# Decode attention on one core: one spread product for a pair of heads, four heads turned at once, and three of eight value parts weighted and folded ahead of the keys' last sum

## The chip, the cores and the metric

The kernel runs on one core of a Trainium2 chip. Its time is the device time of one execution in microseconds (us); the kernel before takes 2681.38 us in the median of three runs (2681.13 to 2682.27). The core has TensorE (PE in the profile, its weight loads PEld), VectorE (DVE), ScalarE (ACT), GpSimd (POOL) and SyncE (SP), which here only issues transfers; 16 DMA engines carry these. SBUF is the large memory on the core, in 128 partitions; TensorE writes its products to banks of PSUM, a second memory.

## The reference, cut to what matters

```python
def _A_ref(x, k_cache, v_cache, wq, wo):        # B=2, Sq=1, D=576, H=32, Sk=8192, Dh=128
    q = (x @ wq).reshape(B, Sq, H, Dh).transpose(0, 2, 1, 3)
    scores = jnp.einsum("bhqd,bhkd->bhqk", q, k_cache) * (Dh ** -0.5)
    p = _softmax(scores, axis=-1)
    o = jnp.einsum("bhqk,bhkd->bhqd", p, v_cache)
    return o.transpose(0, 2, 1, 3).reshape(B, Sq, H * Dh) @ wo

x = x + _A_ref(_layernorm(x), A_k_cache, A_v_cache, A_wq, A_wo)
x = x + _B_ref(_layernorm(x), B_w_gate, B_w_up, B_w_down)      # gated MLP, 4608 wide
x = x + _A_ref(_layernorm(x), A_k_cache, A_v_cache, A_wq, A_wo)
x = x + _B_ref(_layernorm(x), B_w_gate, B_w_up, B_w_down)
```

All is float32. Each of the two attention layers reads the whole key and value caches, 268 MB each, once; with the weights 1152 MB come from HBM in a run.

## The kernel before

**Items and parts.** The work of a layer is a list ITEMS of 30 pairs (two neighbouring heads h, h+1 of one batch entry b) and four single heads at the end. For a pair, the 128 partitions hold 64 stretches of each head, 128 keys to a partition. Keys and values of a pair are 8 parts of 16 rows (a row: 128 numbers of one key in each partition). The first layer takes the items in order, the second in reverse (`seq`), so that the two batch entries of a pair of heads follow each other and some data at the turn is kept.

**Where things lie.** `space` is one SBUF tile of 200 KB a partition, shared out by the class Arena while the program is written: in the long loops there are three places of 8 parts. A list of transfers (`plan_first`, `plan_second`, `plan_mlp`) is fixed in order: keys of item n+1, values of item n, keys of n+2, and so on. `done(key)` gives a part back, and `pump()` issues the next transfers on SP's queue as far as their places are free; on the chip each waits there, in order, for the last reader of its place. A transfer of keys thus waits for the values of an earlier item, and one of values for the keys of the item before.

**One item.** `query(n)` spreads the item's q over the partitions: one TensorE product for each head of the pair, from 4 rows of `qsb` with a column of `pick`, into a PSUM bank (`qb`). `multiply(n, k, m)` takes m parts from part k: VectorE multiplies keys by q (L743, one operand in SBUF, one in the bank), GpSimd adds the upper half of each row's 128 products to the lower (L772). `add_up` sums the 64 left (VectorE, L775) into the scores and gives the keys' parts back. `units(n)` makes three steps of a pair: parts 0 to 2, 3 to 5, 6 and 7 (48, 48 and 32 rows). The last sum of item p, with the search for its maximum (`peak`, L799, a turn on TensorE, L801), stands at the head of the next item's turn in the loop over `seq`. Then `highest` (L807, L809) and `softmax` (ScalarE, L832) write the weights into `prz`, SBUF, one copy for all pairs. `total` and `inverse` make 1 / sum.

**Values.** `values(i)` multiplies four rows of values at a time by their weights on TensorE (L913) into an accumulator in PSUM. For most pairs (`folds(n)`: n from 3 to 26 in the first layer, from 2 to 26 in the second) the last FOLD = 2 of the 8 parts go another way, two items later (item f in the loop): `weigh(f)` adds the two halves of the weights in `prz` into `share` in PSUM (L875, both operands in SBUF), multiplies the parts by them in place (VectorE, L880, one operand in SBUF and one in PSUM) and adds row upon row on GpSimd until four are left (L883). `folded(f)` brings these into the accumulator with one call of a product (L891, two instructions), gives the parts back and with them the place of the values.

**Closing a pair of heads.** After both batch entries (item a in the loop), `gather` takes the diagonal of the accumulator (L927, L928) into the tile `wide`, `context` turns it with four products (L936, two instructions each) into `po`, and `divide` writes the four quotients into `oT`, mostly on ScalarE (L955).

**The order** is written out by hand in the loop over `seq` and is that of every engine's instructions. For a pair it was: last sum and peak of p; weigh(f); first multiply; query of the next item; highest and softmax of p; second multiply; total and inverse; folded(f); gather and context of a; values of p; first sum; third multiply; second sum; divide of a.

**q itself** is made by `q_products` in 9 steps: the 2048 columns of a half row of `wq` go to four strips of 32 partitions, 512 columns each, strip c holding heads 4c to 4c+3 of the 16. A row of a strip is a batch entry and a half of the heads. `spread()` fills `wide` with the pattern that `norm` needs; `home` is an SBUF tile that holds kept rows at the turn of the layers.

Of the kernel before, what the change touches and what calls it, by code (L numbers as in the profile page):

```python
# [15 lines left out]
P = 128  # L16
B = 2
H = 32
SK = 8192
DH = 128  # L20
# [5 lines left out]
HALF = P // 2  # L26

GH = 4
WIDE = (GH, 4 * GH)
NU = 9  # L30
EQ = 512
HG = DF // 16
PAD = 6
# [12 lines left out]
SPLIT = (18, 18, 12, 16)  # L46
FOLD = 2

# [77 lines left out]
def decode_layers(ctx, tc, x_in, kc, vc, wq, wo, wg, wu, wd, out):  # L126
    nc = tc.nc
# [288 lines left out]
    def plan_mlp(layer):  # L416
# [24 lines left out]
    make_identity(nc, ident)  # L441
    sizes = [1, 1, 4, 4, 4, 4, 2, 24, 4]
    few = consts.tile([P, sum(sizes)], F32, name="few")
    unit, mhalf, pick, diag, of, sums, side, owner, strip = [
        few[:, sum(sizes[:k]):sum(sizes[:k + 1])] for k in range(len(sizes))
# [161 lines left out]
    def attention(layer):  # L607
# [4 lines left out]
        def q_products(w, at, to, start, stop):  # L612

            for c in range(4):
                nc.tensor.matmul(
                    acc[32 * c:32 * c + 2 * B, to, :], xt[:, PAD + at:PAD + at + 2 * B], w[:, c, :],
                    start=start, stop=stop,
                )

        def half_products(h):  # L620

            for k in range(4):
                key = ("wq", 1, h, k)
                q_products(
                    ready.pop(key).rearrange("p (c w) -> p c w", w=EQ), 64 * k + 8 + 4 * h, h,
                    k == 0, h == 0 and k == 3,
                )
                done(key)
                if k > 0 if h else k < 3:
                    idle_products(2, 1 - h)  # L630

        if layer == 0:
            for us in GU[0]:
                w = ready.pop(("wq", 0, us[0])).rearrange("p (u c w) -> p u c w", c=4, w=EQ)
                for u in us:
                    q_products(w[:, u - us[0]], 32 * u, 0, u == 0, u == NU - 1)
                done(("wq", 0, us[0]))
        else:
            half_products(1)
            key = ("wq", 1, NU - 1)  # L640
            q_products(ready.pop(key).rearrange("p (c w) -> p c w", w=EQ), 32 * (NU - 1), 1, False, True)
            done(key)
# [5 lines left out]
        seq = list(range(N))[::1 - 2 * layer]  # L648

        def query(n):  # L650

            it = ITEMS[n]
            qps.append(qps.pop(0))
            qb[n] = qps[0]
            for i in range(it.heads):
                h, to = it.h + i, slice(i * HALF, i * HALF + P // it.heads)
                c, r = (h // 4) % 4, h // 16 * B + it.b
                nc.tensor.matmul(  # L658
                    qb[n][to, :], pick[32 * c:32 * c + 4, r:r + 1].to_broadcast([4, P // it.heads]),
                    qsb[32 * c:32 * c + 4, (h % 4) * DH:(h % 4 + 1) * DH], start=True, stop=True,  # L660
                )

# [4 lines left out]
        def at_once(n, k):  # L667

            return layer == 1 and n == seq[0] and k in (0, ITEMS[n].parts - 1)
# [229 lines left out]
        def values(i, lo=0, hi=8):  # L899
# [20 lines left out]
            if left and 4 * hi >= gs and not less:  # L920
                ready.pop(key)

        def gather(n):

            t = osb[n] = wide
            q = accumulator(n).rearrange("p (r d) -> p r d", r=4)
            nc.vector.tensor_tensor(out=q, in0=q, in1=diag.unsqueeze(2).to_broadcast([P, 4, DH]), op=ALU.mult)  # L927
            nc.vector.tensor_reduce(out=t, in_=q.rearrange("p r d -> p d r"), axis=AX.X, op=ALU.add)  # L928

        def context(n):  # L930

            lo = 32 * (ITEMS[n].h % GH)
            t = osb.pop(n)
            for i in range(GH):
                c = 2 * ITEMS[n].heads
                nc.tensor.matmul(po[lo:lo + 32, i, :c], t[:, i::GH], of[:, :c], start=True, stop=True)  # L936

        def divide(n, by_scalar=False):
            it = ITEMS[n]
            lo = 32 * (it.h % GH)  # L940
            if it.heads == 1:
# [6 lines left out]
                )  # L948
                return
            for b, i in ((b, i) for b in range(B) for i in range(2)):  # L950
                to = oT[lo + 32 * i:lo + 32 * i + 32, it.h // GH, :, :, b]
                o = po[lo:lo + 32, :, 2 * b + i:2 * b + i + 1].to_broadcast([32, GH, 2])
# [43 lines left out]
        for i, n in enumerate(seq):  # L996
# [254 lines left out]
```

## Time and profile before

| | before |
|---|---|
| time, median of three runs | 2681.38 us (2681.13 to 2682.27) |
| the profiled execution, span | 2681.6 us, 15416 instructions |
| busy: DVE, POOL, PE, ACT | 1992.5, 1560.5, 885.1, 165.7 us |
| read from HBM | 1152.39 MB, 430 GB/s over the span |
| share of the DMA queue of SP on the 16 engines | 99.7% |
| first attention layer, its long loop | about 45 to 1140 us |
| MLP and the turn to the second layer | about 1285 to 1400 us |
| second attention layer, its long loop | about 1465 to 2541 us |

How to read it. The page gives the busy time of each engine, the span in 40 slices, the DMA queues, the chain of work that ended last and the costliest groups of instructions. A group's line has the kernel's line, the engine, the operation, the tiles written <- read, the shapes and the count; then busy us and the mean ns of one; then the idle time just before them and what ended it. A row of the timeline has its start and its length in us, and in square brackets how long the engine had stood idle and what released it. "DMA share" in a table by windows is the busy share of the 16 DMA engines. The rows for SPq are the requests for transfers at the moment when they leave SP's queue.

### The profile page before, as it was taken

Reading aid. Unit: us, or ns where it says so; the run is one execution under the profiler, and the core shown is the slowest. Engines: PE = TensorE matmul, PEld = TensorE weight load, DVE = VectorE, ACT = ScalarE, POOL = GpSimd, SP = SyncE. Lnnn points to the kernel's source line nnn. Section 1 sums busy time; section 2 is a strip of 40 time slices with the busy share of each in tenths; the row PEclk is TensorE's granted clock in tenths of the full one; section 3 lists DMA queues with packets and bytes.
Section 4 is the critical chain, followed back from the end, with each engine's and each line's share of the span. In section 5 each row is a group of like instructions: output and inputs, shape, how many; then the busy total and the mean of one; then the engine's idle time right before and its main releaser. Section 6 shows DMA issues by size and latency. Waiting matters only on the chain.

```text
span 2681.6 us, 15416 instructions
## 1 busy us (share of the span) xinstructions
PE 885.1 (33%) x6198; PEld 270.4 (10%) x6198; DVE 1992.5 (74%) x907; ACT 165.7 (6%) x792; POOL 1560.5 (58%) x412
## 2 busy tenths in 40 slices
PE   1323332232223232334663323233223323332346
PEld 0000000000000000011221000000000000000022
DVE  4878888888788888867038778878888888888740
ACT  0000000000000000001026000000000000000000
POOL 2546676667666766744028457666766676676620
PEclk8556655665566566566986665566566556655678
DMA  9999999999999999999999999999999999999998
GB/s 422 436 437 427 434 434 431 436 430 435 432 431 433 431 437 433 429 430 427 417 417 426 434 432 432 435 435 430 431 435 433 432 432 435 434 428 434 433 428 378
DMA packets 29344, 1153.41 MB, mean 430 GB/s; under 512 B 3384, under 2 KB 3416, under 8 KB 4184
## 3 DMA queue, kind: packets, MB, share of 16 engines
q1 hardware_dynamic: 29088, 1152.40, 99.7%
q8 instruction: 49, 0.80, 0.1%
q14 instruction: 23, 0.19, 0.0%
q10 hardware_dynamic: 184, 0.02, 0.0%
HBM read 1152.39 MB, written 0.01 MB: 430 GB/s over the span
## 4 chain that ended last, share of the span: by engine, by line
DMA 67%; DVE 20%; PE 8%; POOL 2%; ACT 2%; issue 1%; SPq 0%; POOLq 0%; ACTq 0%; DVEq 0%
DMA space<-in_A_k_cache_dram 60%; DVE space L743 17%; PE acc L891 3%; DMA space<-in_B_w_down_dram 3%; DMA space<-in_B_w_gate_dram 2%; POOL space L772 2%; DVE scores L775 2%; PE bank L658 1%; DMA space<-in_B_w_up_dram 1%; PE bank L809 1%; ACT prz L832 1%; DMA space<-in_A_v_cache_dram 1%; PE bank L845 1%; PE acc L913 0%; PE bank L1210 0%
## 5 line engine op out<-in xcount | busy, mean ns | idle before, releaser
L772 POOL TENSOR_TENSOR space<-space 128x3072 f32<-128x3072 f32 (+4 forms) x221 | 1128.2, 5105 | 461.3 <-DVE space L743 330.9
L743 DVE TENSOR_TENSOR space<-space,bank 128x6144 f32<-128x6144 f32 (+4 forms) x223 | 1111.9, 4987 | 346.1 <-DMA space<-in_A_k_cache_dram 274.6
L775 DVE TENSOR_REDUCE scores<-space 128x48 f32<-128x3072 f32 (+4 forms) x223 | 568.7, 2550 | 93.1 <-POOL space L772 92.9
L913 PE MATMUL acc<-space,prz 128*16 128x512 f32 (+1 forms) x3312 | 513.7, 785 | 353.9 <-DMA space<-in_A_v_cache_dram 342.3
L883 POOL TENSOR_TENSOR space<-space 128x2048 f32<-128x2048 f32 x147 | 398.0, 2708 | 392.6 <-DVE space L880 377.0
L658 PE MATMUL bank<-qsb,few 4*64 4x128 f32 (+1 forms) x256 | 45.5, 433 | 895.0 <-DVE space L743 887.4
L880 DVE TENSOR_TENSOR space<-space,bank 128x4096 f32<-128x4096 f32 x49 | 216.6, 4420 | 1.7
L913 PEld LDWEIGHTS acc<-space,prz 128*16 128x16 f32 (+1 forms) x3312 | 108.7, 117 | 740.3 <-issue 454.0
L824 ACT ACTIVATE nbs<-bank 128x2 f32<-128x2 f32 (+1 forms) x68 | 11.6, 171 | 2012.5 <-PE bank L809 1975.4
L658 PEld LDWEIGHTS bank<-qsb,few 4*64 4x64 f32 (+1 forms) x256 | 20.2, 199 | 914.6 <-DVE space L743 897.9
L580 POOL TENSOR_TENSOR rstd<-ve,few 128x1 f32<-128x1 f32 x4 | 2.2, 551 | 168.3 <-DVE ve L578 168.3
L891 PE MATMUL acc<-space,few 128*16 128x512 f32 x98 | 92.6, 1048 | 0.7 <-POOL space L883 0.7
L801 PE MATMUL bank<-ident,m 128*1 128x128 f32 x68 | 21.1, 310 | 196.5 <-DVE m L799 196.2
L936 PE MATMUL bank<-few,wide 128*32 128x4 f32 (+1 forms) x272 | 20.9, 200 | 170.5 <-DVE wide L928 170.5
L1162 DVE STREAM_TRANSPOSE gu<-acc 128x288 f32<-128x288 f32 x4 | 1.9, 483 | 93.0 <-ACT acc L1160 93.0
L832 ACT ACTIVATE prz<-scores,nbs 64x128 f32<-64x128 f32 (+1 forms) x128 | 50.7, 396 | 11.7 <-POOL prz L822 8.9
L765 ACT ACTIVATE space<-space 128x128 f32<-128x128 f32 x164 | 48.4, 296 | 19.4 <-DVE space L743 16.4
L809 PE MATMUL bank<-m,few 1*128 1x2 f32 (+1 forms) x136 | 38.8, 352 | 26.9 <-DVE m L807 26.9
L584 DVE TENSOR_TENSOR x<-bank,x 128x144 f32<-128x144 f32 x4 | 1.2, 308 | 60.5 <-PE bank L1210 41.5
L927 DVE TENSOR_TENSOR acc<-acc,few 128x512 f32<-128x512 f32 x34 | 23.5, 691 | 26.7 <-PE acc L913 26.7
L936 PEld LDWEIGHTS bank<-few,wide 128*32 128x32 f32 x272 | 19.0, 154 | 216.6 <-issue 211.6
L759 POOL TENSOR_TENSOR space<-space,qs 128x512 f32<-128x512 f32 x23 | 29.2, 1271 | 18.5 <-ACT qs L740 18.5
(106 smaller groups left out, 498.2 us busy)
## 6 DMA issues: line engine op xcount, KB each, us to landing
space<-in_A_v_cache_dram SPq DMA_DIRECT2D x7, 4096.0 KB
space<-in_A_k_cache_dram SPq DMA_DIRECT2D x6, 4096.0 KB
space<-in_B_w_gate_dram SPq DMA_DIRECT2D x9, 1152.0 KB
space<-in_B_w_up_dram SPq DMA_DIRECT2D x9, 1152.0 KB
space<-in_B_w_down_dram SPq DMA_DIRECT2D x8, 1152.0 KB
space<-in_A_wq_dram SPq DMA_DIRECT2D x9, 1024.0 KB
space<-in_A_wo_dram SPq DMA_DIRECT2D x2, 4608.0 KB
space<-in_A_k_cache_dram SPq DMA_DIRECT2D x4, 2048.0 KB
```

Source lines behind the costliest of these rows:

```text
L658: nc.tensor.matmul(qb[n][to, :], pick[32 * c:32 * c + 4, r:r + 1].to_broadcast([4, P // it.heads]), qsb[32 * c:32 * c + 4, (h % 4) * DH:(h ...
L743: nc.vector.tensor_tensor(out=u[:, :r, :], in0=t[:, :r, :], in1=qb[n].unsqueeze(1).to_broadcast([P, r, DH]), op=ALU.mult)
L765: nc.scalar.activation(u[:, j, :], u[:, j, :], AF.Copy, accum_out=S[n][:, base(n, k) + j:base(n, k) + j + 1])
L772: nc.gpsimd.tensor_tensor(out=half, in0=half, in1=u[:, :r, DH // 2:], op=ALU.add)
L775: nc.vector.tensor_reduce(out=S[n][:, base(n, k):base(n, k) + own_rows(n, k, m)], in_=prod.pop((n, k)), axis=AX.X, op=ALU.add)
L809: nc.tensor.matmul(mT[n][:, :heads], ones[0:1, :], m1[:, :heads], start=True, stop=True)
L832: nc.scalar.activation(pr[at, lo:].rearrange("p (g e) -> p g e", e=4)[:, 0:it.rows // 2 * it.heads:2 * it.heads, :], s[at, :it.rows].rearr ...
L880: nc.vector.tensor_tensor(out=t, in0=t, in1=share.unsqueeze(2).to_broadcast([P, rows, DH]), op=ALU.mult)
L883: nc.gpsimd.tensor_tensor(out=t[:, :rows - less], in0=t[:, :rows - less], in1=t[:, less:rows], op=ALU.add)
L891: nc.tensor.matmul(accumulator(n)[0:16, :], owner[:, 8 * ITEMS[n].b:8 * ITEMS[n].b + 16], part_at(arena.live[key, lo][0], 4 * DH), start=F ...
L913: nc.tensor.matmul(accumulator(n)[32 * c:32 * c + m, :], pr[:, at:at + m], t[g // 4][:, g % 4 * 4:g % 4 * 4 + 4, :].rearrange("p j d -> p ...
L936: nc.tensor.matmul(po[lo:lo + 32, i, :c], t[:, i::GH], of[:, :c], start=True, stop=True)
```

## The change

It has four pieces.

1. **q by one product.** The strips of `wq` are read in another order (`by_strips`), so that the two heads of a pair stand in neighbouring strips, in the same columns. The two products of `query` become one over 36 rows (4 of each strip and the 28 between). Its stationary side, which sends the first head to partitions 0 to 63 and the second to 64 to 127, is made by `pairs_of` with two VectorE copies whenever the half of the heads changes (twice in a layer), from the new constant `both`, into `wide` and a third of `home`.
2. **Four heads turned at once.** For heads below 28, `gather` of two neighbouring pairs goes side by side into `home`; `context` runs only at the second of them, with 64 columns where it had 32, and `divide` writes the quotients of both.
3. **Three parts folded.** FOLD is 3: the weighting takes 48 rows where it took 32, GpSimd folds 48 to 24, 12, 8 and 4 rows, and TensorE multiplies five parts instead of six.
4. **The order.** `weigh(f)` stands ahead of the last sum and the peak of p, and `folded(f)` right behind the first multiply and the query.

```diff
-FOLD = 2
+FOLD = 3
...
+    both = both.rearrange("p (r i) -> p r i", i=2)
+    low_rows, high_rows = [
+        ident[:, HALF * q:HALF * (q + 1)].rearrange("p (i z) -> p z i", i=2)[:, :4, :] for q in range(2)
+    ]
+    nc.vector.tensor_add(both, low_rows, high_rows)
...
-                    acc[32 * c:32 * c + 2 * B, to, :], xt[:, PAD + at:PAD + at + 2 * B], w[:, c, :],
+                    acc[32 * c:32 * c + 2 * B, to, :], xt[:, PAD + at:PAD + at + 2 * B], w[:, c // 2, c % 2],
...
+        def by_strips(w):
+
+            return w.rearrange("p (a q m e d) -> p q e a m d", a=2, q=2, m=2, e=2)
...
+        of_batch = [wide, home[:, 2 * P:3 * P]]
+        spread_for = []
+
+        def pairs_of(s):
+
+            if spread_for[-1:] == [s]:
+                return
+            spread_for.append(s)
+            for b, to in enumerate(of_batch):
+                nc.vector.tensor_copy(
+                    to.rearrange("p (i q) -> p i q", i=2), both[:, s * B + b, :].unsqueeze(2).to_broadcast([P, 2, HALF])
+                )
...
-            for i in range(it.heads):
-                h, to = it.h + i, slice(i * HALF, i * HALF + P // it.heads)
-                c, r = (h // 4) % 4, h // 16 * B + it.b
-                nc.tensor.matmul(
-                    qb[n][to, :], pick[32 * c:32 * c + 4, r:r + 1].to_broadcast([4, P // it.heads]),
-                    qsb[32 * c:32 * c + 4, (h % 4) * DH:(h % 4 + 1) * DH], start=True, stop=True,
-                )
+            h, r = it.h, it.h // 16 * B + it.b
+            lo = HALF * (h // 4 % 2) + 32 * (h % 2)
+            m = h // 8 % 2 * 2 + h % 4 // 2
+            if it.heads == 2:
+                rows = slice(lo, lo + 36)
+                pairs_of(it.h // 16)
+                of_row = of_batch[it.b][rows, :]
+            else:
+                rows = slice(lo, lo + 4)
+                of_row = pick[rows, r:r + 1].to_broadcast([4, P])
+            nc.tensor.matmul(qb[n], of_row, qsb[rows, m * DH:(m + 1) * DH], start=True, stop=True)
...
+        def joined(n):
+
+            return ITEMS[n].h < H - GH
+
+        def closes(n):
+
+            return ITEMS[n].h % GH == 2 - 2 * layer
+
         def gather(n):
 
-            t = osb[n] = wide
+            at = ITEMS[n].h % GH * HALF
+            t = osb[n] = home[:, at:at + P] if joined(n) else home[:, :P] if layer else wide
...
+            if joined(n):
+                if not closes(n):
+                    return
+                t = home[:, :2 * P]
+            rows = t.shape[1] // GH
...
-                nc.tensor.matmul(po[lo:lo + 32, i, :c], t[:, i::GH], of[:, :c], start=True, stop=True)
+                nc.tensor.matmul(po[lo:lo + rows, i, :c], t[:, i::GH], of[:, :c], start=True, stop=True)
...
+            if joined(n):
+                if closes(n):
+                    for m in (n, n - B * (1 - 2 * layer)):
+                        divide_pair(m, ITEMS[m].h % GH * 16, by_scalar)
+                return
...
+            if f is not None:
+                weigh(f)
             if first or ahead:
                 add_up(p, *units(p)[-1])
                 peak(p)
-            if f is not None:
-                weigh(f)
...
+                if j == 0 and f is not None:
+                    folded(f)
...
-                    if f is not None:
-                        folded(f)
```

More of the change, by code (lines that the diff above doesn't have):

```diff
@@ L441, in decode_layers @@
     make_identity(nc, ident)
-    sizes = [1, 1, 4, 4, 4, 4, 2, 24, 4]
+    sizes = [1, 1, 4, 4, 4, 4, 2, 24, 4, 8]
     few = consts.tile([P, sum(sizes)], F32, name="few")
-    unit, mhalf, pick, diag, of, sums, side, owner, strip = [
+    unit, mhalf, pick, diag, of, sums, side, owner, strip, both = [
         few[:, sum(sizes[:k]):sum(sizes[:k + 1])] for k in range(len(sizes))
@@ L624, in half_products @@
                 q_products(
-                    ready.pop(key).rearrange("p (c w) -> p c w", w=EQ), 64 * k + 8 + 4 * h, h,
+                    by_strips(ready.pop(key)), 64 * k + 8 + 4 * h, h,
                     k == 0, h == 0 and k == 3,
@@ L640, in attention @@
             key = ("wq", 1, NU - 1)
-            q_products(ready.pop(key).rearrange("p (c w) -> p c w", w=EQ), 32 * (NU - 1), 1, False, True)
+            q_products(by_strips(ready.pop(key)), 32 * (NU - 1), 1, False, True)
             done(key)
@@ L949, in divide, with divide_pair @@
                 return
+            divide_pair(n, lo, by_scalar)
+        def divide_pair(n, lo, by_scalar):
+            it = ITEMS[n]
             for b, i in ((b, i) for b in range(B) for i in range(2)):
-                to = oT[lo + 32 * i:lo + 32 * i + 32, it.h // GH, :, :, b]
+                at = 32 * (it.h % GH + i)
+                to = oT[at:at + 32, it.h // GH, :, :, b]
                 o = po[lo:lo + 32, :, 2 * b + i:2 * b + i + 1].to_broadcast([32, GH, 2])
```

6 lines of the change are left out of this document (3 added, 3 removed).

## The prediction

> **What bounds the kernel now.** I read the table of DMA queues first, then the table by windows, then the groups of instructions by shape, and last the timeline of two neighbouring items (an item is one pair of heads of one batch entry: 8.4 MB of keys, 8.4 MB of values).
>
> ```profile
> HBM read 1152.39 MB, written 0.01 MB: 430 GB/s over the span
> 125.00:1125.00 1000.00, 291.74 (x1636) 80.70 (x1625) 815.64 (x293) 43.52 (x182) 654.92 (x149) 0.59 1.00 433
> 1465.00:2541.00 1076.00, 316.14 (x1772) 87.91 (x1772) 878.00 (x318) 45.83 (x192) 699.93 (x159) 0.59 1.00 433
> 2660.00:2682.00 22.00, 16.65 (x300) 10.04 (x298) 0.31 (x1) 0.00 (x0) 0.00 (x0) 0.88 0.61 255
> ```
>
> In the windows the last two columns are the busy share of the 16 DMA engines and the rate. In both long loops the engines are full, at 433 GB/s: the span is the bytes over the rate, and only the last 22 us fall off (255 GB/s). VectorE is busy 816 of 1000 us, GpSimd 655, TensorE 292. So nothing that makes an engine's work shorter can bring much; a change costs as soon as it makes a request for keys or values come after the queue has run dry. I therefore look for the lead of the requests and for loops between engines that are nearly as long as an item's transfer.
>
> ```profile
> 995.49 6.55 DVE L743 TENSOR_TENSOR space<-space,bank 128x6144 f32<-128x6144 f32 x1 [4.61 <-DMA space<-in_A_k_cache_dram]
> ...
> 1009.31 0.69 DVE L927 TENSOR_TENSOR acc<-acc,few 128x512 f32<-128x512 f32 x1
> ...
> 1010.64 3.34 DVE L775 TENSOR_REDUCE scores<-space 128x48 f32<-128x3072 f32 x1
> 1013.90 4.41 DVE L743 TENSOR_TENSOR space<-space,bank 128x4096 f32<-128x4096 f32 x1
> 1018.23 3.35 DVE L775 TENSOR_REDUCE scores<-space 128x48 f32<-128x3072 f32 x1
> 1018.46 4.54 POOL L772 TENSOR_TENSOR space<-space 128x2048 f32<-128x2048 f32 x1 [2.30 <-DVE space L743]
> 1023.03 2.29 DVE L775 TENSOR_REDUCE scores<-space 128x32 f32<-128x2048 f32 x1 [1.45 <-POOL space L772]
> 1025.34 0.33 SPq L168 DMA_DIRECT2D space<-in_A_v_cache_dram  x1
> 1026.09 0.20 DVE L875 TENSOR_TENSOR bank<-prz 128x32 f32<-128x32 f32 x1 [0.45 <-PE bank L801]
> 1026.32 4.42 DVE L880 TENSOR_TENSOR space<-space,bank 128x4096 f32<-128x4096 f32 x1
> 1030.82 8.29 POOL L883 TENSOR_TENSOR space<-space 128x2048 f32<-128x2048 f32 x3 [7.83 <-DVE space L880]
> 1034.20 6.55 DVE L743 TENSOR_TENSOR space<-space,bank 128x6144 f32<-128x6144 f32 x1 [3.45 <-DMA space<-in_A_k_cache_dram]
> ...
> 1040.67 0.27 DVE L807 TENSOR_REDUCE m<-bank 1x2 f32<-1x128 f32 x1
> 1040.88 6.69 POOL L772 TENSOR_TENSOR space<-space 128x3072 f32<-128x3072 f32 x1 [1.77 <-issue]
> 1041.54 6.55 DVE L743 TENSOR_TENSOR space<-space,bank 128x6144 f32<-128x6144 f32 x1 [0.60 <-PE bank L658]
> 1045.73 0.33 SPq L168 DMA_DIRECT2D space<-in_A_k_cache_dram  x1
> 1048.11 3.32 DVE L775 TENSOR_REDUCE scores<-space 128x48 f32<-128x3072 f32 x1
> 1062.81 0.33 SPq L168 DMA_DIRECT2D space<-in_A_v_cache_dram  x1
> 1072.89 6.55 DVE L743 TENSOR_TENSOR space<-space,bank 128x6144 f32<-128x6144 f32 x1 [4.70 <-DMA space<-in_A_k_cache_dram]
> ```
>
> An item begins when its keys have landed (995.49, 1034.20, 1072.89: 38.69 and 38.71 us apart; I use 38.70) and runs in three units of 48, 48 and 32 rows: VectorE multiplies (L743), GpSimd adds the halves (L772), VectorE sums (L775). Every second item has the gather (L927, then L928) between. The value request goes out the moment the third sum is done (1025.34, 1062.81), the key request when the fold's two products are done (1045.73). The value request of 1025.34 leads the next landing (1034.20) by 8.86 us, that of 1062.81 leads 1072.89 by 10.08; the key requests lead the transfer that they must not miss by about as much. How late may a request be? The first of all, at 0.73, shows the delay to the first bytes with an empty queue; another, at 1440.51, came just too late:
>
> ```profile
> 0.73 7.38 SPq L257 DMA_DIRECT2D space<-in_A_wq_dram  x2
> 1.00:1.70 0.70, 0.00 (x0) 0.00 (x0) 0.35 (x5) 0.00 (x0) 0.29 (x1) 1.00 0.00 0
> 1.70:2.70 1.00, 0.00 (x0) 0.00 (x0) 0.87 (x7) 0.00 (x0) 0.00 (x0) 1.00 2.16 655
> 1440.51 0.33 SPq L168 DMA_DIRECT2D space<-in_A_k_cache_dram  x1
> 1442.00:1443.00 1.00, 0.28 (x2) 0.20 (x2) 1.00 (x1) 0.97 (x7) 1.00 (x1) 1.00 0.94 328
> ```
>
> Nothing moves until 1.70, then at once more than the mean: 1.0 us. After 1440.51 the rate sags to 328 GB/s from 1442 on, 1.5 us later. I take 1.5 us, between 1.0 and 2.
>
> **The change, part by part.** The prices come from the groups by shape (x is the count, then busy us, mean ns):
>
> ```profile
> L743 DVE TENSOR_TENSOR space<-space,bank 128x6144 f32<-128x6144 f32 x114 | 747.2, 6554 | 301.3 <-DMA space<-in_A_k_cache_dram 266.5 <-PE bank L658 34.8
> L743 DVE TENSOR_TENSOR space<-space,bank 128x4096 f32<-128x4096 f32 x61 | 269.0, 4411 | 0.0
> L883 POOL TENSOR_TENSOR space<-space 128x2048 f32<-128x2048 f32 x49 | 220.3, 4496 | 384.9 <-DVE space L880 377.0 <-issue 7.9
> L883 POOL TENSOR_TENSOR space<-space 128x1024 f32<-128x1024 f32 x49 | 115.5, 2356 | 3.8
> L883 POOL TENSOR_TENSOR space<-space 128x512 f32<-128x512 f32 x49 | 62.3, 1271 | 3.9
> L880 DVE TENSOR_TENSOR space<-space,bank 128x4096 f32<-128x4096 f32 x49 | 216.6, 4420 | 1.7
> ```
>
> Three parts instead of two: the weighting L880 grows from 32 to 48 rows, 4.42 to 6.56 us (L743 has both sizes, 6.554 and 4.411). GpSimd's fold goes from 32 > 16 > 8 > 4 rows to 48 > 24 > 12 > 8 > 4. At (4496 - 2356) / 1024 = 2.09 ns an element beyond that, 24 rows cost 6.64 us, 12 rows 3.43, and 4 rows 1.27 twice; with the three gaps of 0.08 (the three now span 8.29, their sum is 8.12) 12.85 us for 8.29. TensorE loses 4 of 24 products of values an item; it waits for landings, so that is worth nothing.
>
> The order: the weighting now stands ahead of the third sum. Now VectorE waits 1.45 us there for GpSimd (row 1023.03), sums, asks for the values and only then weights. After it, the value request is behind L875 and L880, 0.25 + 6.56 us; the waiting request stands at the head of SP's queue with the next key request behind it. The key request, on the other hand, has the fold's products moved up behind the first multiply and comes at about the same place, with 8 us of lead: costed at nothing, its cover the transfer before it. On TensorE the maximum's product L809 is now queued behind the fold's, so the softmax comes some 2 us later; its readers, the products of values, wait for a landing half an item (19 us) after the keys' anyway.
>
> Whether the 1.45 us are filled by the new order decides the sum. L875 adds two slices of prz and would start while the third L772 is still running. No row shows L875 beside a busy GpSimd: its 49 calls come after the third sum, with GpSimd idle. **From below:** it starts at once, as L743 does beside L772 at an unchanged 6.55. **From above:** it is held to the end of L772, as the instruction that stands at that place today is in every item (row 1023.03, there for its data). L743 beside L772 has one operand in SBUF and one in a PSUM bank, L875 both in SBUF; the row nearest in place and time is 1023.03, so I take the upper end and keep the lower as the first rival. The Trainium skill, page "SBUF — State Buffer", section "Who interferes with whom", says that a VectorE instruction with two SBUF inputs contends with a GpSimd instruction that reads SBUF, and that the one that comes second is blocked whole: by that rule the sum is the upper end. The trace agrees only on the harmless side, the 6.55 of L743.
>
> This closes a loop from GpSimd's first half-add to the one of the next item. Held: half-add 6.69; to the first sum 0.03; to the third multiply 3.26 (1010.64 to 1013.90); to its half-add 4.56; that one 4.54; release 0.03; L875 0.25; L880 to fold 4.50 + 2.14 = 6.64; fold 12.85; to the next half-add 0.08: **38.93 us, 0.23 over the 38.70 of an item.** At once: from the third multiply to the end of the second sum 1018.23 + 3.35 - 1013.90 = 7.68 in place of 4.56 + 4.54 + 0.03: 37.48, 1.2 under.
>
> Before the loop costs anything it uses up the lead of the value request. In an item with a gather the first sum starts 15.15 us after the landing; 14.9 with the shorter spread product below. Held, the request follows at 14.9 + 3.26 + 4.56 + 4.54 + 0.03 + 0.25 + 6.47 (1034.20 to 1040.67, a multiply of 48 rows to the next) + 2.31 (1023.03 to 1025.34) = 36.3. It must go by 38.7 - 1.5 = 37.2; 0.9 us are gone after 4 items. L880 has 49 calls, 24 in the first layer and 25 in the second by the bounds of folds(): (24 - 4) + (25 - 4) = 41 items pay 0.23 to 0.24: **+9.6 us.** At once, the request goes at 36.3 - 9.13 + 7.68 = 34.9 and nothing is paid.
>
> The rest. One product of 36 rows for two of 4 rows saves some 0.3 us ahead of the second multiply, which waits for L658; in the loop the first sum waits for GpSimd, so it is worth nothing. Four times a run, at the start of a layer and at its middle, two copies of 128x128 prepare the rows:
>
> ```profile
> L485 DVE COPY wide<-few x3: 216/219/226, 4.3 to 2592.8; 128x128 f32<-128x128 f32 x3
> L936 PE MATMUL bank<-few,wide 128*32 128x4 f32 x240 | 18.4, 200 | 168.1 <-DVE wide L928 168.1
> ```
>
> 0.22 us each, 1.8 in all, under the keys' transfer; bounds, nothing and one half-add of 6.69 each if GpSimd held them off too (a rival below). Turning two pairs at once halves most of the 240 products of 200 ns, on an engine with time to spare; the quotients only bunch, on ScalarE, which is busy 44 of the 1000 us. At the end of the second layer 4 more quotients run on VectorE, under 1 us, while weights are still moving. The strips of wq are read in another order at the same count. All at nothing, the cover being the transfer; without cover under 2 us together.
>
> Sum: 2681.6 (the profiled span; the runs' median is 0.2 below) + 9.6 - 0.2 = **2691.0**.
>
> **The rivals.** (1) *L875 isn't held, or the loop has slack that I don't see:* the order fills GpSimd's wait, the loop is 37.48, the value request leads by 38.7 - 34.9 = 3.8 us, and the full queue hides everything: 2681.4. For it: L743's steady 6.55 beside L772; against: two SBUF operands. The point at which it decides is 1.2 us of hold out of 1.45. (2) *The copies for the spread rows are held as well,* one behind a first half-add, in the middle item of each layer: 6.7 us on VectorE, 2.4 to 5 of them beyond the lead: 5 to 10 more, 2686 to 2701. For it: they come when GpSimd becomes free to start L772; against: L485's 216 to 226 ns, though always beside an idle GpSimd. The same section of that page of the Trainium skill gives such copies a mode that takes the pair of ports; no run here shows it. (3) *Faster:* only the start, the dip at 1442 and the last 22 us are not full, and no part of the change shortens them by 5 us; at most 1 or 2, 2680.
>
> **How the numbers follow.** What a measurement can tell here is about 0.2%, 5.4 us. Held 0.62, for every large row of VectorE beside a busy GpSimd has at most one operand in SBUF, and the one instruction in that place waits; in it the loop lies between 38.86 and 39.1 (gaps and release 0.1 more or less), so 37 to 43 items pay 0.16 to 0.4: 2687 to 2698, and in about one of seven even less than 5.4. Not held 0.31. Copies alone 0.05, faster 0.02. Slower 0.53 + 0.05 = 0.58; same 0.09 + 0.31 = 0.40; faster 0.02. The range must take in both main cases: 2680.5 to 2698; the likeliest one's own is 2687 to 2698.
>
> **What would show it.** In the trace after: L875 starting 0.03 us after the third L772 ends (held) or right behind the second sum (not held); a fold of four instructions spanning 12.85 us; landings 38.9 us apart late in each layer and the rate under 433 GB/s (held), or 38.7 and 433 (not held); value requests under 2 us ahead of the landing. I am wrong if the landings stay at 38.7 though L875 is held (then the fold or the third half-add is shorter than I reckon), or if they stretch without a hold (then a request needs more than 3.8 us).

## The result and the profile after

The changed kernel takes 2723.7 us (median of 5 runs, 2719.53 to 2741.75); the kernel before took 2681.53 beside it (2681.13 to 2682.77). The ratio is 1.0168, with a 95% interval of 1.0151 to 1.0185: slower by some 42 us, where 10 were forecast. (Ratios and their intervals, here and below, are taken over all runs; that of the two medians is 1.0157.) The profiled execution is the longest of the five (2741.75, span 2739.7), so its losses are somewhat above the median's.

The page and the table by windows, for the two long loops (columns as before; the last two are the busy share of the 16 DMA engines and the rate):

```profile
HBM read 1152.39 MB, written 0.01 MB: 421 GB/s over the span
125.00:1125.00 1000.00, 271.20 (x1327) 78.57 (x1319) 872.78 (x289) 41.28 (x173) 741.32 (x168) 0.59 0.99 422
1500.00:2560.00 1060.00, 284.66 (x1411) 83.13 (x1411) 926.57 (x304) 44.45 (x186) 770.32 (x175) 0.59 0.98 420
```

The same bytes, but 422 and 420 GB/s where it was 433. That is the whole loss: 1000 x (1 - 422/433) + 1060 x (1 - 420/433) = 57 us, and the spans differ by 58.1. The time went into the two loops, evenly, and into nothing else.

The groups by shape show that the sizes were read rightly, and that the addition of the two halves is held (its line 875 is 901 now, the weighting 880 is 906, the fold 883 is 909, the half-add 772 is 798, the sum 775 is 801, the multiply 743 is 769, the query's product 658 is 687):

```profile
L909 POOL TENSOR_TENSOR space<-space 128x3072 f32<-128x3072 f32 x49 | 326.5, 6664 | 330.3 <-DVE space L906 323.5 <-issue 6.8
L906 DVE TENSOR_TENSOR space<-space,bank 128x6144 f32<-128x6144 f32 x49 | 321.1, 6554 | 1.7
L909 POOL TENSOR_TENSOR space<-space 128x1536 f32<-128x1536 f32 x49 | 168.6, 3441 | 3.8
L909 POOL TENSOR_TENSOR space<-space 128x512 f32<-128x512 f32 x98 | 124.3, 1268 | 7.7
L901 DVE TENSOR_TENSOR bank<-prz 128x48 f32<-128x48 f32 x49 | 74.5, 1520 | 0.0
```

1520 ns, where L875 took 200 with 32 rows. One item in order, from the timeline of VectorE, GpSimd and SyncE's requests:

```profile
300.19 6.56 DVE L769 TENSOR_TENSOR space<-space,bank 128x6144 f32<-128x6144 f32 x1 [4.76 <-DMA space<-in_A_k_cache_dram]
...
323.02 3.35 DVE L801 TENSOR_REDUCE scores<-space 128x48 f32<-128x3072 f32 x1
323.18 4.55 POOL L798 TENSOR_TENSOR space<-space 128x2048 f32<-128x2048 f32 x1 [2.23 <-DVE space L769]
326.28 1.52 DVE L901 TENSOR_TENSOR bank<-prz 128x48 f32<-128x48 f32 x1
327.83 6.55 DVE L906 TENSOR_TENSOR space<-space,bank 128x6144 f32<-128x6144 f32 x1
334.31 2.28 DVE L801 TENSOR_REDUCE scores<-space 128x32 f32<-128x2048 f32 x1
...
336.61 0.33 SPq L168 DMA_DIRECT2D space<-in_A_v_cache_dram  x1
...
338.88 6.55 DVE L769 TENSOR_TENSOR space<-space,bank 128x6144 f32<-128x6144 f32 x1 [1.97 <-DMA space<-in_A_k_cache_dram]
```

L901 begins behind the second sum, and ends at 327.80, just after the half-add L798 (323.18 + 4.55 = 327.73). The value request goes out 36.42 us after the landing of 300.19 and 2.27 us ahead of the next. What the queue does meanwhile, in windows of 1 us; a packet counts whole in the window where it begins, hence shares over 1:

```profile
333.00:334.00 1.00, 0.00 (x0) 0.00 (x0) 1.00 (x1) 0.00 (x0) 0.00 (x0) 0.50 1.21 524
334.00:335.00 1.00, 0.00 (x0) 0.00 (x0) 1.00 (x2) 0.00 (x0) 0.53 (x1) 0.50 1.21 524
335.00:336.00 1.00, 0.00 (x0) 0.00 (x0) 1.00 (x1) 0.00 (x0) 1.00 (x1) 0.50 0.45 197
336.00:337.00 1.00, 0.04 (x1) 0.04 (x1) 0.87 (x2) 0.00 (x0) 1.00 (x1) 0.50 0.16 66
337.00:338.00 1.00, 0.33 (x1) 0.04 (x1) 0.00 (x0) 0.00 (x0) 1.00 (x1) 0.50 2.33 786
338.00:339.00 1.00, 0.00 (x0) 0.00 (x0) 0.12 (x1) 0.00 (x0) 1.00 (x1) 0.50 0.77 262
```

How long is a packet? The DMA view of the kernel before, from 1020 to 1030, says:

```profile
DMA packets 66, 4.33 MB, mean 433 GB/s; under 512 B 0, under 2 KB 0, under 8 KB 0
```

65.6 KB each, and 16 engines x 10 us / 66 = 2.42 us. So 524 GB/s over a microsecond is 8 packets. From 333 to 335 sixteen begin, the last of the keys on most engines; from 335 to 337 only four. The trace's records of single packets say what the four are: four engines have one more packet of keys to move and end it between 337.91 and 338.52; the other twelve are done between 336.25 and 336.95, the first of them 2.6 us ahead of the landing that VectorE sees at 338.88. The first value packets begin at 337.59, 1.0 us after the request. **The queue runs dry well before the landing**, and a request 2.27 us ahead of it comes too late for twelve of the 16 engines. Eleven value packets begin nearly together, from 337.59 to 337.78, and take 3.0 to 3.3 us each instead of 2.42. So these engines lose some 1.1 us idle and 0.7 on the first packet in the mean, and the next landing is 2.0 us late (40.70 after this one). In this profile the landings behind requests with less than 3.2 us of lead are mostly 40 to 42 us after the one before, the others mostly 38.7 to 39.1.

In the second layer's middle item there is a second thing, from the timeline:

```profile
1961.49 0.97 DVE L668 COPY wide<-few 128x128 f32<-128x128 f32 x1
1962.33 6.65 POOL L798 TENSOR_TENSOR space<-space 128x3072 f32<-128x3072 f32 x1
1962.38 6.68 DVE L668 COPY home<-few 128x128 f32<-128x128 f32 x1
```

A copy that takes 0.22 us elsewhere lasts 6.68 beside a half-add and ends with it; that item and the next are 85.3 us together, 7.9 over two transfers (two items take 79.7 in the mean of this profile). The other three switches of the run did not show it.

### The profile page after: what moved, and what is told of

Same layout as the page of the kernel before. It is cut to its first block, busy times and chain, and to the rows that moved or that the text cites. A ratio compares the mean times of both kernels' runs of the same rounds, so it can differ in the third digit from the quotient of the medians.

```text
span 2739.7 us, 14166 instructions
## 1 busy us (share of the span) xinstructions
PE 849.8 (31%) x5574; PEld 269.5 (10%) x5574; DVE 2164.2 (79%) x916; ACT 165.5 (6%) x792; POOL 1779.3 (65%) x461
## 4 chain that ended last, share of the span: by engine, by line
DMA 45%; DVE 34%; POOL 13%; PE 5%; issue 3%; ACT 1%; POOLq 0%; another core or an unknown queue 0%; SPq 0%; DVEq 0%; ACTq 0%
DMA space<-in_A_k_cache_dram 38%; DVE space L769 18%; POOL space L909 10%; DVE scores L801 7%; DVE space L906 5%; DMA space<-in_B_w_down_dram 2%; POOL space L798 2%; DMA space<-in_B_w_gate_dram 2%; PE acc L917 2%; DVE bank L901 1%; DMA space<-in_B_w_up_dram 1%; PE bank L687 1%; DVE acc L962 1%; DMA space<-in_A_wo_dram 1%; DVE home L963 1%
## 5 line engine op out<-in xcount | busy, mean ns | idle before, releaser
L798 POOL TENSOR_TENSOR space<-space 128x3072 f32<-128x3072 f32 (+4 forms) x221 | 1126.9, 5104 | 354.7 <-DVE space L769 317.6
L909 POOL TENSOR_TENSOR space<-space 128x3072 f32<-128x3072 f32 x196 | 619.4, 3160 | 341.8 <-DVE space L906 323.5
L939 PE MATMUL acc<-space,prz 128*16 128x512 f32 (+1 forms) x2920 | 465.3, 801 | 447.2 <-DMA space<-in_A_v_cache_dram 433.4
L906 DVE TENSOR_TENSOR space<-space,bank 128x6144 f32<-128x6144 f32 x49 | 321.1, 6554 | 1.7
L939 PEld LDWEIGHTS acc<-space,prz 128*16 128x16 f32 (+1 forms) x2920 | 97.4, 119 | 757.6 <-issue 462.6
L687 PE MATMUL bank<-qsb,home 36*128 36x128 f32 x60 | 23.4, 492 | 294.6 <-DVE space L769 276.1
L687 PE MATMUL bank<-qsb,wide 36*128 36x128 f32 x60 | 23.1, 486 | 274.3 <-DVE space L769 261.2
L901 DVE TENSOR_TENSOR bank<-prz 128x48 f32<-128x48 f32 x49 | 74.5, 1520 | 0.0
L687 PEld LDWEIGHTS bank<-qsb,home 36*128 36x128 f32 x60 | 14.8, 305 | 304.5 <-DVE space L769 284.8
L976 PE MATMUL bank<-few,home 128*64 128x4 f32 (+2 forms) x136 | 17.1, 249 | 85.6 <-DVE home L963 85.6
```

Of the source, the lines that this page charges most:

```text
L687: nc.tensor.matmul(qb[n], of_row, qsb[rows, m * DH:(m + 1) * DH], start=True, stop=True)
L798: nc.gpsimd.tensor_tensor(out=half, in0=half, in1=u[:, :r, DH // 2:], op=ALU.add)
L901: nc.vector.tensor_tensor(out=share.rearrange("p (g e) -> p g e", e=4), in0=pr[:, 0], in1=pr[:, 1], op=ALU.add)
L906: nc.vector.tensor_tensor(out=t, in0=t, in1=share.unsqueeze(2).to_broadcast([P, rows, DH]), op=ALU.mult)
L909: nc.gpsimd.tensor_tensor(out=t[:, :rows - less], in0=t[:, :rows - less], in1=t[:, less:rows], op=ALU.add)
L939: nc.tensor.matmul(accumulator(n)[32 * c:32 * c + m, :], pr[:, at:at + m], t[g // 4][:, g % 4 * 4:g % 4 * 4 + 4, :].rearrange("p j d -> p ...
```

## The experiments

Three theories. **A**, the prediction's: the loop between the engines, 38.93 us against 38.70, sets the pace. **B**: a request less than about 4 us ahead of the next landing lets the engines run dry, however long the loop is. **C**: the third part, the moved products or the copies cost by themselves. Each kernel was timed beside the kernel before on the same chip; ratios are to that.

**The hold taken away.** One half of the weights is copied to the bank by ScalarE first, so that VectorE's addition has one operand in SBUF:

```diff
-nc.vector.tensor_tensor(
-    out=share.rearrange("p (g e) -> p g e", e=4), in0=pr[:, 0], in1=pr[:, 1], op=ALU.add
-)
+both_halves = share.rearrange("p (g e) -> p g e", e=4)
+nc.scalar.copy(both_halves, pr[:, 1])
+nc.vector.tensor_tensor(out=both_halves, in0=pr[:, 0], in1=both_halves, op=ALU.add)
```

> The changed kernel, but the two halves of the weights are added with one operand in SBUF only: ScalarE copies one half into the bank first, VectorE then adds the other half to it. Theory A (the loop between the engines sets the pace, 38.93 us with the hold, some 37.5 without): no hold, so no cost, 2681 to 2683. Theory B (a value request that goes out with less than about 4 us ahead of the next keys' landing lets the queue run dry, and each such request costs some 2 to 3 us, however long the loop is): the addition takes 0.2 to 0.3 us instead of 1.52, the requests of the items with a gather go out about 1.3 us earlier, 3.6 us instead of 2.3 ahead; that is still at the edge, so part of the loss stays: 2683 to 2700. The copies held in a layer's middle item may remain, up to 8 us more. Theory C (the hold costs nothing; three parts in themselves or the moved products cost): 2715 to 2725.

Measured: 2702.76 us, ratio 1.0084 (1.0067 to 1.0101). From this kernel's timeline (the addition is L903):

```profile
1044.51 6.55 DVE L769 TENSOR_TENSOR space<-space,bank 128x6144 f32<-128x6144 f32 x1 [3.70 <-DMA space<-in_A_k_cache_dram]
...
1066.24 4.56 POOL L798 TENSOR_TENSOR space<-space 128x2048 f32<-128x2048 f32 x1 [0.97 <-DVE space L769]
1069.34 0.20 DVE L903 TENSOR_TENSOR bank<-prz,bank 128x48 f32<-128x48 f32 x1
1069.58 6.55 DVE L906 TENSOR_TENSOR space<-space,bank 128x6144 f32<-128x6144 f32 x1
...
1078.35 0.33 SPq L168 DMA_DIRECT2D space<-in_A_v_cache_dram  x1
...
1083.22 6.55 DVE L769 TENSOR_TENSOR space<-space,bank 128x6144 f32<-128x6144 f32 x1 [4.58 <-DMA space<-in_A_k_cache_dram]
```

0.20 us in the middle of the half-add: the second SBUF operand was the cause of the hold. The request is 1.3 us earlier in items with a gather (35.1 after the landing for 36.4; 33.84 here, in one without). Half of the loss is gone, not all: theory A, by which nothing should be left, falls, and with it the prediction's first rival, whose case this is. Theory B's own range ended at 2700, 2.8 us too low.

**The copies on ScalarE**, alone and together with the first edit:

```diff
-                nc.vector.tensor_copy(
+                nc.scalar.copy(
```

> The changed kernel, but the two copies that prepare the rows of a spread query run on ScalarE. If the hold of the copy in the second layer's middle item (6.68 us in the profile, that item and the next 7.9 us too long) costs what the trace suggests: 6 to 10 us less than the changed kernel, 2712 to 2718. If the transfer would have run dry there anyway: no difference, 2720 to 2725.

> Both edits: no addition and no copy with two SBUF operands beside GpSimd. Theory A: 2681 to 2683. Theory B: as the first run, less what the copies cost, 2681 to 2692. Theory C: 2710 to 2718.

Measured: 2726.84 us, 1.0171 (1.0146 to 1.0197), and 2705.71, 1.0088 (1.0073 to 1.0103). Neither is distinguishable from the kernel that it was made from. Both miss their ranges: the first is 1.8 us above the upper one, the second lies between theory B's 2692 and theory C's 2710. The held copy is real where it happens, but no cost of it shows in the times; in the profiles of the first edit and of the two-part kernels below, whose copies stay on VectorE, they all take 0.22 us.

**Two parts in the new order**, with the hold and without it (FOLD = 3 becomes 2; the second has the first experiment's edit as well):

> The changed kernel with two parts instead of three folded, all else in the new order, so the addition is still held to the end of the third half-add. The weighting is 2.1 us shorter (4.42 instead of 6.55), so the value request goes out 2.1 us earlier, 4.4 us ahead of the next landing in the items with a gather, and the loop between the engines is some 32.2 us. Theory A: 2681 to 2683, plus up to 8 for a held copy. Theory B: a lead of 4.4 us is just enough: 2682 to 2690. Theory C with the moved products, not the third part, as the cause: 2700 or more. In every case the addition still takes about 1.5 us in the trace.

> The changed kernel with two parts and with the addition's one operand from the bank: the query's one product, the fold's products behind the next item's first multiply and the weighting ahead of the keys' last sum all stay. The request leads by about 5.6 us in items with a gather. Theory B: nearly no loss, 2681 to 2686. Theory C (the moved products or the query's product cost something by themselves): 2690 or more.

Measured: 2692.18 us, 1.0034 (1.0023 to 1.0046), and 2681.98, 1.0002 (0.9992 to 1.0011). In the first the addition takes 1575 ns, held as before, and the time is 2 us above what theory B expected at that lead. The second kernel has the query's one product, the turned pairs, the moved products and the weighting ahead of the last sum, and is as fast as the kernel before; its windows over the two loops are full again:

```profile
125.00:1125.00 1000.00, 298.63 (x1524) 85.92 (x1516) 810.67 (x295) 46.98 (x202) 654.08 (x149) 0.59 1.00 433
1465.00:2541.00 1076.00, 321.03 (x1672) 92.95 (x1672) 873.92 (x321) 50.51 (x217) 703.10 (x161) 0.59 1.00 433
```

So nothing of these edits costs by itself, and C falls but for what the third part does to the request.

**Only the request delayed.** The kernel before, with ScalarE scaling a used-up part of the keys in place behind the third sum, so that the request must wait (1792 and 2816 for 768 in the other two):

```diff
     key = name("k", layer, n)
+    if n < PAIRS and (k, m) == (6, 2) and several(n):
...
+        for lo, hi in [(0, 4096), (0, 768)]:
+            nc.scalar.activation(flat[:, lo:hi], flat[:, lo:hi], AF.Copy, scale=...)
```

> The kernel before; only the value request of each folded item waits for two scalings by ScalarE of a part of the keys that is already used up (4096 and 768 elements, some 4.5 us), so that it leads the next landing by about 4.4 us in items with a gather and 5.6 in the others, instead of 8.86 and 10.08. The order between VectorE and GpSimd, the addition and the fold are those of before. Theory A (only the loop between the engines counts): no cost, 2681 to 2683. Theory B (the lead counts): about what the new order with two parts cost at the same lead, 2682 to 2694.

> The same with 4096 and 1792 elements, some 5.5 us: leads of about 3.4 and 4.6 us. Theory A: 2681 to 2683. Theory B: as the changed kernel without the hold, whose leads are 3.6 and 4.9: 2698 to 2710.

> The same with 4096 and 2816 elements, some 6.5 us: leads of about 2.4 and 3.6 us, those of the changed kernel. Theory A: 2681 to 2683. Theory B: the changed kernel's whole loss, 2715 to 2730, though no loop between engines is longer than before.

Measured: 2699.32 us, 1.0068 (1.0053 to 1.0083); 2706.61, 1.0095 (1.0080 to 1.0110); 2721.71, 1.0144 (1.0127 to 1.0161). The first lies above its range (its lead came out at 4.1, not 4.4), the other two within. From the third one's timeline:

```profile
300.08 6.55 DVE L743 TENSOR_TENSOR space<-space,bank 128x6144 f32<-128x6144 f32 x1 [5.83 <-DMA space<-in_A_k_cache_dram]
...
329.96 6.38 ACT L786 ACTIVATE space<-space,scores 128x4096 f32<-128x4096 f32 x2 [12.77 <-DVE scores L775]
336.37 0.33 SPq L168 DMA_DIRECT2D space<-in_A_v_cache_dram  x1
338.85 6.55 DVE L743 TENSOR_TENSOR space<-space,bank 128x6144 f32<-128x6144 f32 x1 [3.49 <-DMA space<-in_A_k_cache_dram]
...
380.13 6.55 DVE L743 TENSOR_TENSOR space<-space,bank 128x6144 f32<-128x6144 f32 x1 [6.66 <-DMA space<-in_A_k_cache_dram]
```

A request 2.48 us ahead of the landing at 338.85, and the next landing 41.28 us later. Two parts, no hold, nothing reordered, and nearly the changed kernel's whole loss. **This is what shows theory B.** In order of the lead that the request of an item with a gather has on a landing that comes in time (38.70 less its offset in the timeline):

| kernel | request after the landing, us | lead, us | median, us | ratio |
|---|---|---|---|---|
| before | 29.9 | 8.8 | 2681.4 | 1 |
| two parts, no hold | 33.0 | 5.7 | 2681.98 | 1.0002 |
| two parts, held | 34.4 | 4.3 | 2692.18 | 1.0034 |
| before, 4.5 us late | 34.6 | 4.1 | 2699.32 | 1.0068 |
| three parts, no hold | 35.1 | 3.6 | 2702.76 | 1.0084 |
| before, 5.5 us late | 35.4 | 3.3 | 2706.61 | 1.0095 |
| before, 6.5 us late | 36.3 | 2.4 | 2721.71 | 1.0144 |
| the change | 36.4 | 2.3 | 2723.7 | 1.0168 |

And item by item, over 507 pairs of neighbouring landings in the profiles of these kernels and of the two with the copies moved: how far the landing after the next comes beyond 38.70 us, by the request's lead on the next one.

| lead, us | items | mean loss, us | middle half of them |
|---|---|---|---|
| under 2.6 | 42 | 2.11 | 1.4 to 2.8 |
| 2.6 to 3.3 | 40 | 1.17 | 0.5 to 1.8 |
| 3.3 to 3.8 | 49 | 0.99 | 0.4 to 1.6 |
| 3.8 to 4.3 | 52 | 0.75 | 0.3 to 1.0 |
| 4.3 to 4.8 | 32 | 0.30 | 0 to 0.5 |
| 4.8 to 6 | 124 | 0.13 | 0 to 0.2 |
| over 6 | 168 | 0.09 | 0 |

A late landing gives the next request more lead, for the engines keep their time: so in the changed kernel late and good items alternate, and about every second item pays some 2 us.

Two things stand beside the lead. In items without a gather the request goes out 1.2 to 1.3 us earlier in every kernel of the first table but the changed one, where it goes out at 36.2, nearly as late as with a gather: there the loop between the engines holds it. The kernel before, 6.5 us late, has no such loop and loses nearly as much; what is between the two ratios, some 6 us and within their intervals, can be this. And the first engine to finish the keys does so 2.5 to 3.4 us ahead of the landing in the mean of one profile, 0.8 to 5.2 in single items, so kernels with the same lead need not lose the same.

**Does the loop cost anything besides?** First a loop that is plainly too long: three parts in the old order (FOLD = 3 in the kernel before).

> The kernel before with three parts folded, everything else in the old order: the sum and the request first, then the addition, the weighting of 48 rows and the fold. Nothing is held and the request keeps its lead of 8.9 us and more, but the loop of the engines is some 42.0 us (38.93 less the hold's 1.3, plus the 1.45 us of VectorE's wait, the sum's 2.31 and 0.6 of rest), 3.3 over an item's transfer. Theory A and theory B both: some 41 to 49 items pay it, 2810 to 2845. If even so long a loop is hidden: 2681 to 2690, and then no loop in this kernel costs anything.

Measured: 2820.18 us, 1.0518 (1.0502 to 1.0534). GpSimd's timeline, first half-adds, and the windows of a stretch:

```profile
607.67 13.35 POOL L772 TENSOR_TENSOR space<-space 128x3072 f32<-128x3072 f32 x2
...
649.60 13.36 POOL L772 TENSOR_TENSOR space<-space 128x3072 f32<-128x3072 f32 x2
...
691.51 13.37 POOL L772 TENSOR_TENSOR space<-space 128x3072 f32<-128x3072 f32 x2
```

```profile
250.00:1200.00 950.00, 234.67 (x1219) 74.62 (x1223) 775.21 (x261) 37.92 (x159) 689.17 (x159) 0.58 0.95 401
```

41.93 and 41.91 us from one to the next, back to back with the fold; (2820.2 - 2680.9) / (41.93 - 38.70) = 43 items that pay it in full. A loop over the transfer does cost, so the question for 38.93 is real. It was asked with the request taken out of the way: the changed kernel, hold and three parts as they are, the values requested in two pieces.

```diff
+    load(begun[6], n, src, 6, 8)
...
+    if arena.clear(lo, 6 * PART):
...
+        load(lo, n, src, 0, 6)
```

> The changed kernel, hold and loop as they are; only the values of a folded item are requested in two pieces: 96 of the 128 rows as soon as the second sum has freed their place, some 10 us earlier than now, and the last 32 rows after the third sum, when the first piece still has more than 5 us to move. Theory B (what costs is the late request alone): 2681 to 2685, plus up to 8 if a copy is held in a middle item. Theory A (the loop of 38.93 us between the engines sets the pace once it is over the transfer's 38.70): 2688 to 2694. In both the addition still takes some 1.5 us.

> The same with the two copies for a spread query on ScalarE. If a copy is held in a middle item and nothing else covers it: up to 8 us less than the run before it. If it isn't held there, or covered: the same within 2 us.

Measured: 2687.29 us, 1.0021 (1.0012 to 1.0030), and with the copies on ScalarE 2688.99, 1.0028 (1.0017 to 1.0039). The timeline of the first (the same code 23 lines further down: the multiply is L792, the half-add L821, the addition L924):

```profile
1005.53 13.38 POOL L821 TENSOR_TENSOR space<-space 128x3072 f32<-128x3072 f32 x2
...
1023.50 1.48 DVE L924 TENSOR_TENSOR bank<-prz 128x48 f32<-128x48 f32 x1
1023.62 10.51 SPq L168 DMA_DIRECT2D space<-in_A_v_cache_dram  x2
...
1036.23 6.55 DVE L792 TENSOR_TENSOR space<-space,bank 128x6144 f32<-128x6144 f32 x1 [2.14 <-DMA space<-in_A_k_cache_dram]
...
1044.49 13.39 POOL L821 TENSOR_TENSOR space<-space 128x3072 f32<-128x3072 f32 x2
...
1083.07 6.71 POOL L821 TENSOR_TENSOR space<-space 128x3072 f32<-128x3072 f32 x1
```

The addition is held as ever (1.48 us), the first piece goes out 12.61 us ahead of the landing, and 36 of the 42 us are gone. The loop is 38.96 us in the item with a gather and 38.58 in the other, 38.77 in the mean. The 6 us that are left could be the loop's or the pieces', whose packets are shorter; the control is the kernel before with the same pieces.

> The control for the run with the request in two pieces: the kernel before, unchanged but for the same two pieces (49 items). In that run the landings were 38.78 us apart instead of 38.70, and the pieces' packets took 614.9 + 1819.4 ns against 2423.0 ns for one whole packet, 11.3 ns more, eight times an item on each DMA engine: 0.09 us. If the pieces themselves cost the difference: 49 times 0.09, 2685 to 2688, as the changed kernel in pieces, and the loop of 38.93 costs nothing. If the loop costs it: 2681 to 2682.

> The control again. In the run before this one the first piece went into the place of older values instead of the place of the keys, so the second piece waited at the head of the queue for the fold's products, with the next key request behind it: that cost 28 us and says nothing of the loop. Here the pieces go where they go in the changed kernel: 96 rows behind the second sum, 32 behind the third. If the pieces' longer packets cost the 6 us of the changed kernel in pieces (47 items times 0.09 us, and a little): 2685 to 2688, and the loop of 38.93 us costs nothing. If its loop costs them: 2681 to 2682.

Measured: the first 2709.45 us, 1.0110 (1.0093 to 1.0127), the second 2686.21, 1.0017 (1.0008 to 1.0026). The first misses its range and is no control: its pieces went into the place of older values. Its requests, and below them one of the second kernel's:

```profile
1028.93 27.93 SPq L168 DMA_DIRECT2D space<-in_A_v_cache_dram  x2
1056.92 0.42 SPq L168 DMA_DIRECT2D space<-in_A_k_cache_dram  x1
```

```profile
1023.22 4.05 SPq L168 DMA_DIRECT2D space<-in_A_v_cache_dram  x2
```

In the first the second piece follows by nearly 28 us, and the key request stands behind it, late too. In the second it follows by some 4 us, as it should. This control costs 4.8 us, the changed kernel in pieces 6.4; the 1.6 between them are less than the 0.2% that can be told apart. The landings agree: they are 38.78 us apart in the control, whose loop is short, and 38.78 in the changed kernel in pieces. So the pieces cost most of the 6 us. What a loop of 38.77 would cost over a transfer of 38.70 these two runs can't show, for in pieces the transfer takes as long as the loop; 0.07 us on 41 items would be some 3 us of the 42.

## What the prediction had right, and the step that failed

- *What bounds the kernel, and that a change costs when a request comes after the queue has run dry:* right. The whole loss is a rate of 421 instead of 433 GB/s in the loops.
- *Sizes:* right. Weighting 6.55 us for 6.56; the fold spans 12.86 to 12.89 for 12.85.
- *The addition held to the end of the third half-add:* right, and shown by the first experiment. It takes 1.52 us because it starts early and waits inside, where the prediction let it start late. Beside the same half-add it takes 0.20 us with one operand in SBUF and 1.52 with two. The rule of the Trainium skill, page "SBUF — State Buffer", section "Who interferes with whom", that of two such instructions the second is blocked whole, agrees with these rows.
- *The request at 36.3 us after a landing:* right, 36.42.
- ***"It must go by 38.7 - 1.5 = 37.2":* this is the step that failed.** The 1.5 us were taken from two rows and counted back from the landing. The first row, 1.0 us from a request to the first packet of an empty queue, came true here. The second, 328 GB/s in the window from 1442, was read as a request that came too late, but packets count where they begin, and a single window in the full loop of the same kernel shows as little:

```profile
335.00:336.00 1.00, 0.00 (x0) 0.00 (x0) 0.00 (x0) 0.00 (x0) 1.00 (x1) 0.50 0.76 328
```

What the 1.5 us left out is that the engines do not end together when VectorE sees the landing: they move packets of 2.42 us out of phase, and the first has no more keys 2.6 us ahead of it in the item above, 2.5 to 3.4 in the means of the profiles. With the 1.0 us from request to first packet a request needs some 3.5 to 4.4 us. The second table says nearly the same: little loss from about 4.8 us on, 2.1 us under 2.6. That the two parts add up in this way is a reading of the packets; what the runs show is the price by lead. The deadline was some 34 us after the landing, not 37.2, and the request at 36.4 paid from the start instead of from the fifth item.

- *The loop of 38.93 us, 0.23 on 41 items, +9.6:* mis-sized, and not the main cost. It is 38.96 with a gather, 38.58 without, 0.07 over in the mean; that would be 3 us, which no run here shows or excludes. So slower was the right word, but the sum behind it priced the loop. The landings don't stretch to an even 38.9 us, as it said, but come at some 38.7 and 40 to 42 in turn. The sum's small gaps were some 0.35 us too long together, and it left the gather out, which puts 0.4 back in every second item (from the first half-add to the first sum 7.12 us with it, 6.73 without).
- *Rival 1, no hold and therefore 2681.4:* wrong for the same reason. Not held, the kernel takes 2702.8 us. The prediction had reckoned a lead of 3.8 us for that case and held it to be enough; its own last sentence named what would prove it wrong, a request that needs more than 3.8 us.
- *Rival 2, the copies held as well:* the mechanism was seen once (6.68 us for 0.22), a cost of it in the times was not.
- *At nothing: the key request, the fold's products behind the multiply, the turned pairs, the quotients:* right, by the two-part kernel without the hold, which keeps them all at 1.0002. The 0.3 us of the shorter query product did not come: two products of 36 rows now span 0.79 us where four of 4 rows spanned 0.69, and the second multiply waits 0.69 us for them instead of 0.60. It is worth nothing either way.

## What to carry to other kernels

Where transfers set the pace, put a price on the lead of every request, and count it back from when the first DMA engine runs out of packets, not from when an engine of the core sees the data: here that made the difference between 1.5 and some 4 us. An edit that delays a request can be tested without the edit, by delaying that request alone in the old kernel. And where a request must come late because only the last piece of its place is not free, asking for the free part early takes away most of the loss, for the price of the shorter packets (here 36 of 42 us for about 5).

## What the runs showed of the hardware

- A VectorE addition with both operands in SBUF was blocked beside GpSimd's addition from its start to that one's end (1.52 us; 0.20 with one operand in a bank), while GpSimd's instruction kept its time (4.55 us beside the held addition, 4.54 before). A copy from SBUF to SBUF that began as GpSimd's half-add did was held in the same way, once (6.68 us for 0.22).
- With only the value request delayed, the kernel's time rose to 1.0068 at 4.1 us of lead, 1.0095 at 3.3 and 1.0144 at 2.4; leads of 5.7 and more cost nothing that the times show (1.0002).
- After a late request the first packets of the engines that had run dry began together and took 3.0 to 3.3 us instead of 2.42.
- The same rows moved in packets of 48 and 16 KB instead of one of 64 took some 1819 + 615 ns instead of 2423 on an engine (means in the traces), 0.5% more, and the landings were 38.78 us apart instead of 38.70 in both kernels that asked in pieces.
